# The second part of a fused attention and feed-forward kernel: its last six groups of 256 tokens become three of 512

## The chip, the cores and the metric

The kernel runs on one core of a Trainium2 chip. The metric is the device time of one execution in microseconds (us). Three runs of the kernel before took 733.32, 734.24 and 737.19 us; the median is 734.24. Besides these there is one profiled execution, whose trace is read here. In the trace PE is TensorE's matmul row, PEld its weight loads, DVE is VectorE, ACT ScalarE, POOL GpSimd, SP the engine that issues the DMAs.

## The reference

Causal softmax attention over 4 batches of 8 heads with 576 tokens of 64 is mixed, by a gate per head, with a read-out of a memory matrix. The result, 2304 tokens of 512, goes through a feed-forward layer with a rational activation:

```python
local = softmax(causal(q @ k.T / 8)) @ v
mem_out = (phi(q) @ M_prev) / (phi(q) @ z_prev + 1e-6)      # phi(x) = elu(x) + 1
x = g * mem_out + (1 - g) * local                            # 2304 x 512
h = x @ w_in                                                 # 2304 x 2048
P = a[0] + a[1] * h + a[2] * h**2 + a[3] * h**3
Q = 1.0 + abs(b[0]) * abs(h) + abs(b[1]) * h**2
out = (P / (Q + 1e-6)) @ w_out                               # 2304 x 512
```

## The kernel before, in words

**Precision.** Operands of the large products are split into a high and a low part of a rounded 32-bit type (hi and lo), and a product is three matmuls: hi by hi, hi by lo, lo by hi. The weights arrive as 64-bit floats. `weights` (line 941) turns one 128-row block of a weight, read as pairs of 32-bit words, into hi and lo: an Abs on ScalarE (line 981) into a buffer `wa`, a clamp on VectorE (983), a shift into a PSUM bank (985), a sign step (987), a step that adds the low word's bits and writes a second buffer `wu` (990), then a rounding copy to hi (`rnd`, lines 530 to 532) and a subtraction to lo (`tt`, 519 or 520).

**Two parts of the feed-forward layer.** d_ff is 2048, which is 16 blocks of 128 (the code calls a block `f`). The first part handles blocks 0 to 5 for all nine groups of 256 tokens while attention is still running, and stores the partial sums in DRAM (`po`) and the split tokens in DRAM (`xh`). The second part handles blocks 6 to 15 for the same nine groups; it loads the tokens again (`xagain`, line 1055), and adds the stored partial sum at the end (line 1155). Its weights lie in SBUF that attention gives back; their conversion can begin only then.

**A group.** `group` (line 1073) takes two blocks at a time. `ffn1` (1061) computes h for one block: 12 matmuls with 256 columns (four pieces of d_model by three products) into half of a PSUM bank, so that one bank holds two blocks of 256 tokens. `act_chain` (1003) then works on the full 512 columns: Abs and a linear step on ScalarE, the denominator on GpSimd, Ln and Exp on ScalarE, products on VectorE; it leaves the activation as `gh` and `gl`. `ffn2` (1067) multiplies each 128 tokens of it by w_out: three matmuls with 512 columns. In the second part the groups 0 and 1 take turns, block pair by block pair (`TURNS = 2`), and the others follow one by one.

**The order.** Nothing loops at run time. Every operation is entered in `Sched` with a cost, its reads and writes and a priority; `place` (line 183) puts one after another: of those that can start, the one with the earliest planned start, and of equal starts the one with the lowest priority number. An engine executes its instructions in that order. `c_mm` (line 65) is the planner's price of a matmul. Buffers are counted by tags: `h2` and `o2` allow four PSUM banks for h and four for outputs in the second part, `w` one for conversion; `xg2` has two token buffers, of which one exists as soon as attention has ended and the other as soon as the first part has; `pi` has two buffers for partial sums, `wa2` and `wu2` two each. All DMAs are issued by SP in planned order.

**Priorities in the second part.** A group's chain has 2,000,000 + 5000 per group, its w_in matmuls 4000 less (5000 less in the last group), so that they run ahead as far as the four banks allow; a weight block has 2,000,000 + 5000 per block number, behind the chains of the first groups.

Of the kernel before, what the change touches and what calls it, by code (L numbers as in the profile page):

```python
# [10 lines left out]
F32R = mybir.dt.float32r  # L11
# [51 lines left out]


def c_mm(n, m=128):
    return max(0.4453 * n + 4.0, 0.93 * m)


def c_mm4(n):
# [247 lines left out]
def tile_attention_ffn(  # L317
# [40 lines left out]
    def rb(x):  # L358
        return x.bitcast(F32)
# [101 lines left out]
    for i in range(2):  # L461
        sc.tag(f"g1{i}", 1).free = []

    w1i = [[w1p.tile([128, KC, 128], F32R, name=f"w1i{hl}{f}") for f in range(F0)] for hl in range(2)]
    w1o = [[w1p.tile([128, DM], F32R, name=f"w1o{hl}{f}") for f in range(F0)] for hl in range(2)]
    tags(ffp, "ta", N["ta"], [128, 512])
    tags(ffp, "tb", N["tb"], [128, 512])
    tags(ffp, "tw", N["tw"], [128, 512])
# [472 lines left out]
    def weights(f, wi, wo, p, t3=("xf", "ta", "tw")):  # L941

        for n, dst in (("i", wi), ("o", wo)):
# [17 lines left out]
                return words(), src[1][f * 128:(f + 1) * 128, :]  # L961
            dma(pair, [], [(raw, None)], p, 128 * 2048 * e)
            if wide:
                wa, wu = sc.buf(t3[1]), sc.buf(t3[2])

                def hi32(words=words):
                    return words()[:, 1:1024:2]

                def lo32(words=words):
                    return words()[:, 0:1024:2]  # L970

                def ai(wa=wa):
                    return wa.t.bitcast(I32)

                def ui(wu=wu):
                    return wu.t.bitcast(I32)
                wp = sc.buf("bk", "w")

                def pi(wp=wp):
                    return wp.t.bitcast(I32)  # L980
                act(c_act(512, False), lambda wa=wa, hi32=hi32: A.activation(wa.t, hi32().bitcast(F32), AF.Abs),
                    [(raw, None)], [(wa, None)], p)
                dve(335, lambda wa=wa: V.tensor_scalar(wa.t, wa.t, E_MIN, E_MAX, op0=ALU.max, op1=ALU.min), [], [(wa, None)], p, "1")  # L983

                dve(c_dve(512), lambda ai=ai, pi=pi: V.tensor_scalar(pi(), ai(), 3, 0x3FFFFFF8, op0=ALU.logical_shift_left,
                                                                     op1=ALU.bitwise_and), [(wa, None)], [(wp, None)], p)
                dve(c_dve(512) + 60, lambda pi=pi, hi32=hi32: V.scalar_tensor_tensor(  # L987
                    out=pi(), in0=hi32(), scalar=-(1 << 30), in1=pi(), op0=ALU.bitwise_and, op1=ALU.bitwise_or),
                    [(raw, None)], [(wp, None)], p)
                dve(c_dve(512) + 60, lambda lo32=lo32, ui=ui, pi=pi: V.scalar_tensor_tensor(  # L990
                    out=ui(), in0=lo32(), scalar=29, in1=pi(), op0=ALU.logical_shift_right, op1=ALU.bitwise_or),
                    [(raw, None), (wp, None)], [(wu, None)], p)
                src = wu
            else:
                src = raw
# [56 lines left out]
        dma(lambda: (xh[t0 // 256], rb(xg.t)), [(xg, None)], [(ex("xh"), t0)], p, 128 * KC * 2048)  # L1052
        return xg

    def xagain(tg, t0, p):

        xg = sc.buf(tg)
        dma(lambda: (rb(xg.t), xh[t0 // 256]), [(ex("xh"), t0)], [(xg, None)], p, 128 * KC * 2048)
        return xg

    def ffn1(hb, e, xg, f, p):
        def g():
            return [(hb.t[:, 256 * e:256 * e + 256], WI[wl][f][:, c, :], xg.t[:, xl, c], x == 0 and c == 0, x == 2 and c == KC - 1)
                    for x, (wl, xl) in enumerate([(0, 0), (0, 1), (1, 0)]) for c in range(KC)]
        mm(g, 3 * KC * c_mm(256), [(xg, None), (ex(("wi", f, 0)), None), (ex(("wi", f, 1)), None)], [(hb, e)], p)

# [5 lines left out]

    def group(ts, fs, th, to, tf, tg, p, ahead):

        xg = [(xload(tf, tg, t0, p - 500) if tf else xagain(tg, t0, p - 500)) for t0 in ts]
        ob = [[sc.buf("bk", to) for _ in range(2)] for _ in ts]
        for m in range(0, len(fs), 2):
            for x, o in zip(xg, ob):
# [54 lines left out]
    f_op.deps.update(f1_ops)  # L1133
    f_op.frees = []
    tag2("xf2", N["xf2"], [128, KC, 256], F32, sc.tags["xf"].tiles)
    tag2("xg2", 1, [128, 2, KC, 256], F32R, sc.tags["xg"].tiles)
    tag2("pi", N["pi"], [128, DM])
    tag2("wa2", N["wa2"], [128, 512])
    tag2("wu2", N["wa2"], [128, 512])
    FP2 = 2e6  # L1140
    for f in range(F0, NF):
        weights(f, lambda hl, f=f: WI[hl][f], lambda hl, f=f: WO[hl][f], W2_PRI + pr["w2"] * f, ("xf2", "wa2", "wu2"))
    sc.late(w2_from, LATE["w2"])

    turns = min(TURNS, NG1)
    for g in range(NG1 - turns + 1):
        ts = [256 * x for x in (range(turns) if g == 0 else [g + turns - 1])]
        t0 = ts[0]
        p = FP2 + 5000 * (t0 // 256)
        ob = group(ts, list(range(F0, NF)), "h2", "o2", None, "xg2", p, pr["ahead2" if g < NG1 - turns else "last"])  # L1150
        for ti in range(2 * len(ts)):
            r = t0 + 128 * ti
            pi = sc.buf("pi")
            dma(lambda pi=pi, r=r: (pi.t, po[r:r + 128, :]), [(ex("po"), r)], [(pi, None)], p, 128 * 2048)
            dve(c_dve(512), lambda pi=pi, o=ob[ti]: V.tensor_tensor(out=pi.t, in0=o.t, in1=pi.t, op=ALU.add),
                [(ob[ti], None)], [(pi, None)], p + 900)
            dma(lambda pi=pi, r=r: (out[r:r + 128, :], pi.t), [(pi, None)], [], p + 900, 128 * 2048)
# [6 lines left out]
        PLAN.extend((o.eng, o.start, o.fin - o.lat, o.idx) for o in sc.ops)  # L1164


TURNS = 2

FULL = 6
PLAN = None  # L1170
# [50 lines left out]
```

## Time and profile before

| what | value |
|---|---|
| median of three runs | 734.24 us |
| profiled execution, its own time | 736.42 us |
| its span (first to last instruction) | 734.6 us |
| TensorE matmuls: busy, instructions | 664.3 us (90%), 4113 |
| VectorE | 590.4 us (80%), 1371 |
| ScalarE | 506.5 us (69%), 1121 |
| GpSimd | 461.4 us (63%), 558 |
| mean granted TensorE clock, share of full | 0.981 |
| DMA traffic | 102.56 MB, mean 140 GB/s |

A busy time is the union of the instructions' spans on one engine. Matmuls overlap in the pipeline, so that the duration of one is longer than its distance to the next one's start. The difference between the execution's time and its span lies ahead of the first and behind the last instruction.

### The profile page before, as it was taken

To read this page: it belongs to the slowest core of one execution; us is meant where nothing else is said; L and a number is where in the kernel's file an instruction comes from. 1 tells how busy PE (TensorE), PEld (TensorE's weight loads), DVE (VectorE), ACT (ScalarE), POOL (GpSimd) and SP (SyncE) were. 2 spreads that over 40 slices of the span, in tenths; PEclk is the share of its full clock that TensorE was granted. 3 is DMA by queue.
4 is the path that set the end of the run, shared out by engine and by line. 5 is a ranking of instruction groups with operands and counts; after the bars stand their busy time and mean duration, and the time that the engine had idled before them with its cause. 6 is when DMAs were issued, how large, how long until landed. Compare 5 with 4: busy or idle time off the path is not lost.

```text
span 734.6 us, 12896 instructions
## 1 busy us (share of the span) xinstructions
PE 664.3 (90%) x4113; PEld 578.9 (79%) x4113; DVE 590.4 (80%) x1371; ACT 506.5 (69%) x1121; POOL 461.4 (63%) x558
## 2 busy tenths in 40 slices
PE   3778788998989998889999999878899999999997
PEld 2656567887886777679889998767798998998996
DVE  5787877798999998789789999899775766657674
ACT  3756778789988899879666686575463854755762
POOL 3566656767765786656545887777753745645663
PEclk9999999999999999999999999999999999999999
DMA  6888687846679766764275443612342212212102
GB/s 152 178 202 216 138 204 180 235 112 191 157 168 236 188 162 157 219 159 104 80 260 161 169 159 106 242 61 87 116 124 91 72 62 83 87 58 72 45 9 79
DMA packets 102580, 102.56 MB, mean 140 GB/s; under 512 B 67632, under 2 KB 80432, under 8 KB 100208
## 3 DMA queue, kind: packets, MB, share of 16 engines
q1 hardware_dynamic: 102512, 101.73, 49.7%
q8 instruction: 33, 0.54, 0.3%
q14 instruction: 35, 0.29, 0.1%
HBM read 52.27 MB, written 23.59 MB: 103 GB/s over the span
## 4 chain that ended last, share of the span: by engine, by line
PE 51%; DVE 17%; ACT 11%; DMA 8%; issue 4%; POOL 4%; SPq 4%; DVEq 0%; ACTq 0%; POOLq 0%
PE bk L492 48%; SPq L485 4%; DMA xf<-in_moe_w_in_dram 3%; PE bk L503 3%; DVE bk L704 2%; ACT Ps L708 2%; DVE g L545 2%; ACT P L708 1%; DVE bk L525 1%; DVE gh L525 1%; ACT g L539 1%; DVE bk L987 1%; POOL tw L519 1%; DVE wa L983 1%; DVE wu L990 1%
## 5 line engine op out<-in xcount | busy, mean ns | idle before, releaser
L492 PEld LDWEIGHTS bk<-xg,w2i 128*128 128x128 f32 x1080 | 133.7, 193 | 6.5 <-DVE gl L1038 1.9
L492 PE MATMUL bk<-xg,w2i 128*128 128x256 f32 x1080 | 135.0, 284 | 3.3 <-DVE gl L1038 1.7
L492 PE MATMUL bk<-w2o,gh 128*128 128x512 f32 x360 | 113.3, 396 | 2.9 <-DVE gl L1038 2.9
L1014 ACT ACTIVATE ta<-bk 128x512 f32<-128x512 f32 x72 | 42.9, 596 | 86.7 <-PE bk L492 84.6
L1018 POOL TENSOR_SCALAR tw<-ta,cb 128x512 f32<-128x512 f32 x60 | 48.5, 808 | 83.5 <-ACT ta L1014 83.3
L519 POOL TENSOR_TENSOR tw<-tw,gh 128x512 f32<-128x512 f32 x54 | 70.6, 1307 | 40.6 <-DVE gh L525 39.6
L519 POOL TENSOR_TENSOR tw<-tw,ta 128x512 f32<-128x512 f32 x68 | 89.3, 1316 | 3.8 <-ACT tw L1019 0.3
L492 PE MATMUL bk<-xg,w1i 128*128 128x256 f32 x648 | 84.0, 284 | 0.2
L704 DVE CUSTOM_DVE_ANT_0 bk<-bk,mk 128x512 f32<-128x512 f32 (+3 forms) x144 | 72.7, 518 | 13.4 <-PE bk L492 11.9
L492 PEld LDWEIGHTS bk<-xg,w1i 128*128 128x128 f32 x648 | 80.9, 191 | 2.5 <-DVE g L545 0.8
L492 PEld LDWEIGHTS bk<-w2o,gh 128*128 128x128 f32 x360 | 67.1, 191 | 15.9 <-DVE gl L1038 3.1
L492 PE MATMUL bk<-w2o,gl 128*128 128x512 f32 x180 | 71.6, 398 | 5.7 <-DVE gl L1038 5.7
L1023 DVE TENSOR_TENSOR tb<-bk,tb 128x512 f32<-128x512 f32 x72 | 49.3, 684 | 33.0 <-ACT tb L1015 31.6
L1022 ACT ACTIVATE ta<-tw,lnb 128x512 f32<-128x512 f32 x72 | 52.0, 724 | 32.1 <-POOL tw L519 28.3
L492 PE MATMUL bk<-qk 128*128 128x128 f32 (+3 forms) x256 | 65.5, 360 | 4.3 <-DVE g L545 1.2
L492 PE MATMUL bk<-w1o,gh 128*128 128x512 f32 x216 | 68.7, 399 | 0.0
L525 DVE SCALAR_TENSOR_TENSOR gh<-bk,ca,ta 128x512 fp32r<-128x512 f32 x72 | 53.5, 743 | 18.4 <-ACT ta L1027 15.3
L525 DVE SCALAR_TENSOR_TENSOR bk<-bk,ca,tw 128x512 f32<-128x512 f32 x72 | 54.1, 751 | 14.4 <-POOL tw L519 13.9
L1015 ACT ACTIVATE tb<-bk,ca 128x512 f32<-128x512 f32 x72 | 55.7, 775 | 0.1
L1025 DVE SCALAR_TENSOR_TENSOR bk<-tb,ca,bk 128x512 f32<-128x512 f32 x72 | 53.8, 748 | 1.9 <-ACT ta L1014 1.0
L716 POOL TENSOR_SCALAR st<-st,g 128x1 f32<-128x1 f32 x78 | 24.0, 308 | 48.7 <-ACT Ps L708 41.4
L708 ACT ACTIVATE Ps<-bk,st 128x128 f32<-128x128 f32 (+2 forms) x96 | 46.0, 483 | 10.9 <-DVE st L704 8.1
(152 smaller groups left out, 1623.4 us busy)
## 6 DMA issues: line engine op xcount, KB each, us to landing
qk<-tt SPq DMA_DIRECT2D x32, 384.0 KB, 4.8
xh<-xg SPq DMA_DIRECT2D x9, 1024.0 KB, 4.7
xg<-xh SPq DMA_DIRECT2D x9, 1024.0 KB, 4.8
xf<-in_moe_w_in_dram SPq DMA_DIRECT2D x16, 512.0 KB, 4.4
qk<-tt SPq DMA_DIRECT2D x32, 256.0 KB, 3.6
xf<-in_moe_w_out_dram SPq DMA_DIRECT2D x16, 512.0 KB, 4.8
xs<-x SPq DMA_DIRECT2D x16, 288.0 KB, 2.7
xf<-xs SPq DMA_DIRECT2D x9, 512.0 KB, 5.8
```

Source lines behind the costliest of these rows:

```text
L485: SY.dma_start(out=o, in_=i)
L492: T.matmul(o, lhsT=l, rhs=r, start=s0, stop=s1, skip_group_check=more)
L519: opts = {"pool": ("pool", c_pool2(n), lambda: G.tensor_tensor(**kw()), "t"), "dve": ("dve", c_dve(n), lambda: V.tensor_tensor(**kw()), "2")}
L525: return dve(c_dve(n) + 61 * ap, lambda: V.scalar_tensor_tensor(out=out(), in0=in0(), scalar=scalar() if callable(scalar) else scalar, in1 ...
L704: V.tensor_tensor_reduce(out=s, in0=s, in1=m, scale=-0.125, scalar=st.t[:, 0:1] if x else 3.0e38, op0=ALU.add, op1=ALU.min, accum_out=st.t ...
L708: act(c_act(w, ap=2), lambda bk=bk, w=w, x=x, c0=c0: A.activation(P.t[:, c0:c0 + w], bk.t[:, 0:w], AF.Exp, bias=st.t[:, mx:mx + 1], scale= ...
L1014: act(c_act(N), lambda: A.activation(a_(), h(), AF.Abs), [(hb, None)], [(ta, None)], p)
L1015: sc.op([("act", c_act(N, ap=2), lambda: A.activation(b_(), h(), AF.Identity, scale=ca[:, 3:4], bias=ca[:, 2:3])), ("dve", c_dve(N) + 61, ...
L1018: sc.op([("pool", c_pool(N, 2), lambda: G.tensor_scalar(w_(), a_(), cb[:, 1:2], cb[:, 0:1], op0=ALU.mult, op1=ALU.add), "s"), ("act", c_ac ...
L1022: act(c_act(N, False, 1), lambda: A.activation(a_(), w_(), AF.Ln, scale=2.0 ** -63, bias=lnb[:, 0:1]), [(tw, None)], [(ta, None)], p)
L1023: dve(c_dve(N), lambda: V.tensor_tensor(out=b_(), in0=h(), in1=b_(), op=ALU.mult), [(hb, None)], [(tb, None)], p)
L1025: dve(c_dve(N) + 61, lambda: V.scalar_tensor_tensor(out=h(), in0=b_(), scalar=ca[:, 1:2], in1=h(), op0=ALU.add, op1=ALU.mult), [(tb, None) ...
```

## The change

Of the second part's nine groups, the first three stay narrow (`NARROW = 3`) and the other six become three of 512 tokens. A wide group takes one block at a time: `ffn1w` computes h for 512 tokens with 12 matmuls of 512 columns, whose moving operand is two pieces of 256, into a whole bank, and four `ffn2` follow into four output banks. Its tokens lie in three buffers `xg2` of two 1 MB loads each, which are views of `w1`, now one tile; the loads also wait for the last converted weight. Narrow groups use `xg1`. The fixed turns of groups 0 and 1 are gone. In the weights' conversion of the second part `wu` and `wa` become one buffer (two of them in all), and `pi` has four. The planner's price of a matmul changes for every matmul of the kernel. The priority of the last group's w_in matmuls (`last`) is no longer used, since the last group starts at number 7.

```diff
 def c_mm(n, m=128):
-    return max(0.4453 * n + 4.0, 0.93 * m)
+    return max(0.418 * n + 13.0, 0.93 * m)
...
-    w1i = [[w1p.tile([128, KC, 128], F32R, name=f"w1i{hl}{f}") for f in range(F0)] for hl in range(2)]
-    w1o = [[w1p.tile([128, DM], F32R, name=f"w1o{hl}{f}") for f in range(F0)] for hl in range(2)]
+    w1 = w1p.tile([128, F0, 2, 2, DM], F32R, name="w1")
+    w1i = [[w1[:, f, hl, 0].rearrange("p (c f) -> p c f", c=KC) for f in range(F0)] for hl in range(2)]
+    w1o = [[w1[:, f, hl, 1] for f in range(F0)] for hl in range(2)]
...
-                wa, wu = sc.buf(t3[1]), sc.buf(t3[2])
+                wa = sc.buf(t3[1])
+                wu = wa if t3[2] == t3[1] else sc.buf(t3[2])
...
-    def xagain(tg, t0, p):
+    def xagain(tg, t0, n, p):
         xg = sc.buf(tg)
-        dma(lambda: (rb(xg.t), xh[t0 // 256]), [(ex("xh"), t0)], [(xg, None)], p, 128 * KC * 2048)
+        for e in range(n):
+            dma(lambda e=e: (rb(xg.t[:, e]), xh[t0 // 256 + e]), [(ex("xh"), t0 + 256 * e)] + [(ex(("wo", NF - 1, 1)), None)] * (n - 1), [(xg, e)], p, 128 * KC * 2048)
         return xg
+    def ffn1w(hb, xg, f, p):
+        def g():
+            return [(hb.t.rearrange("p (a b) -> p a b", a=2), WI[wl][f][:, c, :], xg.t[:, :, xl, c], x == 0 and c == 0, x == 2 and c == KC - 1)
+                    for x, (wl, xl) in enumerate([(0, 0), (0, 1), (1, 0)]) for c in range(KC)]
+        mm(g, 3 * KC * c_mm(512), [(xg, None), (ex(("wi", f, 0)), None), (ex(("wi", f, 1)), None)], [(hb, None)], p)
+    def wide_group(t0, n, fs, th, to, tg, p, ahead):
+        x = xagain(tg, t0, n, p - 500)
+        o = [sc.buf("bk", to) for _ in range(2 * n)]
+        for m in range(0, len(fs), 3 - n):
+            hb = sc.buf("bk", th)
+            if n == 2:
+                ffn1w(hb, x, fs[m], p + pr["chain"] * m - ahead)
+            else:
+                for e in range(2):
+                    ffn1(hb, e, x, fs[m + e], p + pr["chain"] * m - ahead, 0)
+            gh, gl = act_chain(hb, 512, p + pr["chain"] * m, True)
+            for k in range(4):
+                f = fs[m + (k // 2 if n == 1 else 0)]
+                ffn2(o[k % (2 * n)], gh, gl, 128 * k, f, f == fs[0], f == fs[-1], p + pr["chain"] * m)
+        return o
...
-    tag2("xg2", 1, [128, 2, KC, 256], F32R, sc.tags["xg"].tiles)
-    tag2("pi", N["pi"], [128, DM])
+    tag2("xg1", 1, [128, 1, 2, KC, 256], F32R, [x.unsqueeze(1) for x in sc.tags["xg"].tiles])
+    tag2("xg2", 0, [128, 2, 2, KC, 256], F32R,
+         [w1[:, 2 * i:2 * i + 2].rearrange("p f h n d -> p (f h n d)").rearrange("p (e h c s) -> p e h c s", e=2, h=2, c=KC)
+          for i in range(F0 // 2)])
+    tag2("pi", 4, [128, DM])
     tag2("wa2", N["wa2"], [128, 512])
-    tag2("wu2", N["wa2"], [128, 512])
...
-        weights(f, lambda hl, f=f: WI[hl][f], lambda hl, f=f: WO[hl][f], W2_PRI + pr["w2"] * f, ("xf2", "wa2", "wu2"))
+        weights(f, lambda hl, f=f: WI[hl][f], lambda hl, f=f: WO[hl][f], W2_PRI + pr["w2"] * f, ("xf2", "wa2", "wa2"))
...
-    turns = min(TURNS, NG1)
-    for g in range(NG1 - turns + 1):
-        ts = [256 * x for x in (range(turns) if g == 0 else [g + turns - 1])]
-        t0 = ts[0]
+    for g in list(range(NARROW)) + list(range(NARROW, NG1, 2)):
+        t0, n = 256 * g, 1 if g < NARROW else 2
         p = FP2 + 5000 * (t0 // 256)
-        ob = group(ts, list(range(F0, NF)), "h2", "o2", None, "xg2", p, pr["ahead2" if g < NG1 - turns else "last"])
+        ob = wide_group(t0, n, list(range(F0, NF)), "h2", "o2", f"xg{n}", p, pr["ahead2" if g < NG1 - 1 else "last"])
...
-TURNS = 2
+NARROW = 3
```

## Rows read from the trace of the kernel before

**Rows 1.** the chain that ended last, 515 to 735: start us, us, what.

```profile
522.55 1.29 POOL w2o L519
523.85 0.77 POOL tw L1018
...
531.86 199.01 PE bk L492 x1258
...
730.89 0.69 DVE pi L1155
```

**Rows 2.** the windows of core 0: busy us (x instructions) by engine, clock, DMA.

```profile
467.00:532.00 65.00, 53.17 (x314) 46.05 (x313) 58.23 (x89) 37.69 (x60) 50.53 (x48) 0.95 0.36 124
532.00:731.00 199.00, 198.85 (x1258) 180.52 (x1258) 133.52 (x196) 115.82 (x179) 110.68 (x98) 1.00 0.21 70
...
480.00:520.00 40.00, 32.81 (x189) 28.53 (x187) 39.68 (x61) 22.58 (x36) 30.21 (x29) 0.96 0.17 54
```

**Rows 3.** groups by line and shape, 532 to 730: busy us, mean ns, idle before.

```profile
L492 PE MATMUL bk<-xg,w2i 128*128 128x256 f32 x816 | 100.6, 283 | 0.0
...
L492 PE MATMUL bk<-w2o,gh 128*128 128x512 f32 x292 | 90.4, 391 | 0.0
L492 PE MATMUL bk<-w2o,gl 128*128 128x512 f32 x147 | 57.4, 391 | 0.9 <-DVE gl L1038 0.9
```

**Rows 4.** the timeline of TensorE at 537 to 549: start us, us, instructions.

```profile
537.23 11.68 PE L492 MATMUL bk<-xg,w2i 128*128 128x256 f32 x96
548.74 0.63 PE L492 MATMUL bk<-w2o,gh 128*128 128x512 f32 x2
```

**Rows 5.** the same timeline at 719 and 730.

```profile
719.13 0.62 PE L492 MATMUL bk<-w2o,gh 128*128 128x512 f32 x2
...
730.01 0.62 PE L492 MATMUL bk<-w2o,gh 128*128 128x512 f32 x2
```

**Rows 6.** the same timeline at 527.

```profile
527.34 3.11 PE L492 MATMUL bk<-xg,w2i 128*128 128x256 f32 x24 [1.31 <-DMA xg<-xh]
```

**Rows 7.** the timeline of all engines, 651 to 664, one activation chain.

```profile
651.63 0.69 DVE L1038 TENSOR_TENSOR gl<-bk,ta 128x512 fp32r<-128x512 f32 x1
...
652.48 0.60 ACT L1014 ACTIVATE ta<-bk 128x512 f32<-128x512 f32 x1 [3.30 <-PE bk L492]
...
661.85 0.68 DVE L1038 TENSOR_TENSOR gl<-bk,ta 128x512 fp32r<-128x512 f32 x1
```

**Rows 8.** timelines of ScalarE, VectorE, GpSimd, 465 to 535: weights being converted.

```profile
477.35 0.68 ACT L981 ACTIVATE wa<-xf 128x512 f32<-128x512 f32 x1 [3.15 <-DMA xf<-in_moe_w_in_dram]
...
480.56 0.69 ACT L981 ACTIVATE wa<-xf 128x512 f32<-128x512 f32 x1
...
506.88 0.67 ACT L981 ACTIVATE wa<-xf 128x512 f32<-128x512 f32 x1
...
515.43 0.68 ACT L981 ACTIVATE wa<-xf 128x512 f32<-128x512 f32 x1 [3.91 <-DVE bk L985]
...
517.44 0.68 DVE L985 TENSOR_SCALAR bk<-wa 128x512 int32<-128x512 int32 x1
...
519.56 0.69 DVE L985 TENSOR_SCALAR bk<-wa 128x512 int32<-128x512 int32 x1
...
500.73 1.30 POOL L519 TENSOR_TENSOR w2i<-wu,w2i 128x512 fp32r<-128x512 f32 x1
...
514.37 1.30 POOL L519 TENSOR_TENSOR w2i<-wu,w2i 128x512 fp32r<-128x512 f32 x1
...
518.31 1.30 POOL L519 TENSOR_TENSOR w2o<-wu,w2o 128x512 fp32r<-128x512 f32 x1
```

**Rows 9.** the line that issues DMAs, 520 to 530.

```profile
L485 SPq DMA_DIRECT2D xg<-xh x2: 327/327/327, 522.6 to 524.0; - x2
...
DMA to landing us min/median/max: 4.6/5.5/6.4
```

**Rows 10.** TensorE's waits, 467 to 532: us in total, times, longest us.

```profile
PE bk L492 <- DVE gl L1038: 10.3, 5, 2.9
```

More of the change, by code (lines that the diff above doesn't have):

```diff
@@ L1053, in xload, with ffn1 @@
         return xg
-    def xagain(tg, t0, p):
+    def xagain(tg, t0, n, p):
         xg = sc.buf(tg)
-        dma(lambda: (rb(xg.t), xh[t0 // 256]), [(ex("xh"), t0)], [(xg, None)], p, 128 * KC * 2048)
+        for e in range(n):
+            dma(lambda e=e: (rb(xg.t[:, e]), xh[t0 // 256 + e]), [(ex("xh"), t0 + 256 * e)] + [(ex(("wo", NF - 1, 1)), None)] * (n - 1), [(xg, e)], p, 128 * KC * 2048)
         return xg
-    def ffn1(hb, e, xg, f, p):
+    def ffn1w(hb, xg, f, p):
         def g():
-            return [(hb.t[:, 256 * e:256 * e + 256], WI[wl][f][:, c, :], xg.t[:, xl, c], x == 0 and c == 0, x == 2 and c == KC - 1)
+            return [(hb.t.rearrange("p (a b) -> p a b", a=2), WI[wl][f][:, c, :], xg.t[:, :, xl, c], x == 0 and c == 0, x == 2 and c == KC - 1)
[16 more added lines that the diff above has]
+        return o
+    def ffn1(hb, e, xg, f, p, half=None):
+        def g():
+            x_ = xg.t if half is None else xg.t[:, half]
+            return [(hb.t[:, 256 * e:256 * e + 256], WI[wl][f][:, c, :], x_[:, xl, c], x == 0 and c == 0, x == 2 and c == KC - 1)
                     for x, (wl, xl) in enumerate([(0, 0), (0, 1), (1, 0)]) for c in range(KC)]
@@ L1073, in group @@
     def group(ts, fs, th, to, tf, tg, p, ahead):
-        xg = [(xload(tf, tg, t0, p - 500) if tf else xagain(tg, t0, p - 500)) for t0 in ts]
+        xg = [xload(tf, tg, t0, p - 500) for t0 in ts]
         ob = [[sc.buf("bk", to) for _ in range(2)] for _ in ts]
@@ L1135, in tile_attention_ffn @@
     tag2("xf2", N["xf2"], [128, KC, 256], F32, sc.tags["xf"].tiles)
-    tag2("xg2", 1, [128, 2, KC, 256], F32R, sc.tags["xg"].tiles)
-    tag2("pi", N["pi"], [128, DM])
+    tag2("xg1", 1, [128, 1, 2, KC, 256], F32R, [x.unsqueeze(1) for x in sc.tags["xg"].tiles])
[3 more added lines that the diff above has]
+    tag2("pi", 4, [128, DM])
     tag2("wa2", N["wa2"], [128, 512])
-    tag2("wu2", N["wa2"], [128, 512])
     FP2 = 2e6
     for f in range(F0, NF):
-        weights(f, lambda hl, f=f: WI[hl][f], lambda hl, f=f: WO[hl][f], W2_PRI + pr["w2"] * f, ("xf2", "wa2", "wu2"))
+        weights(f, lambda hl, f=f: WI[hl][f], lambda hl, f=f: WO[hl][f], W2_PRI + pr["w2"] * f, ("xf2", "wa2", "wa2"))
     sc.late(w2_from, LATE["w2"])
-    turns = min(TURNS, NG1)
-    for g in range(NG1 - turns + 1):
-        ts = [256 * x for x in (range(turns) if g == 0 else [g + turns - 1])]
-        t0 = ts[0]
+    for g in list(range(NARROW)) + list(range(NARROW, NG1, 2)):
+        t0, n = 256 * g, 1 if g < NARROW else 2
         p = FP2 + 5000 * (t0 // 256)
-        ob = group(ts, list(range(F0, NF)), "h2", "o2", None, "xg2", p, pr["ahead2" if g < NG1 - turns else "last"])
-        for ti in range(2 * len(ts)):
+        ob = wide_group(t0, n, list(range(F0, NF)), "h2", "o2", f"xg{n}", p, pr["ahead2" if g < NG1 - 1 else "last"])
+        for ti in range(2 * n):
             r = t0 + 128 * ti
```

## The prediction

> **What bounds the kernel now.** I read from the page to the end of the kernel and then backwards. The busy shares on the page name no single engine, since they are means over stages. The chain of waits does [rows 1]: it ends in one unbroken piece of 199.01 us on TensorE, 531.86 to 730.86, and before that it runs through VectorE, GpSimd and ScalarE. The windows say the same from outside [rows 2]: from 532 to 731 TensorE is busy 198.85 of 199.00 us at full clock, VectorE only 133.52; from 480 to 520 VectorE is busy 39.68 of 40 us and TensorE waits. So the kernel has three stages for this question: up to about 480 the first part and attention; then the conversion of the second part's weights, which VectorE sets; then 199 us that TensorE alone sets. What is saved in TensorE's columns of the last stage comes off the time; what is late in the stage before moves all of it.
>
> The last stage is matmuls of two kinds [rows 3]: 816 with 256 columns (x by w_in) and 292 + 147 with 512 (g by w_out). Mean durations there (283 and 391 ns) overlap and are no price. The price is the distance of starts. 96 of the first kind begin at 537.23 and the next kind at 548.74 [rows 4]: 11.51/96 = 119.9 ns. Of the second, 48 lie between 719.13 and 730.01 [rows 5]: 10.88/48 = 226.7 ns. The records agree: 816 x 0.1199 + 439 x 0.2267 = 197.4 of the 198 us of that view.
>
> **The change, part by part.** *Wide matmuls.* Six groups of 256 tokens, ten blocks of d_ff, 12 matmuls each: 720 with 256 columns become 360 with 512. All 720 lie in TensorE's own stage: seven groups' worth is 840, the first 24 of those run at 527.34 [rows 6] and 816 behind 532 [rows 3]; the changed groups are the last six of the seven. 720 x 119.9 = 86.3 us, 360 x 226.7 = 81.6 us: 4.7 us less. No row has a moving operand in two pieces of 256; the bounds are 226.7 ns (the other 512-column matmul, the same engine and columns, so not less) and 2 x 119.9 = 239.8 (nothing saved). I take 226.7, the nearest in shape.
>
> *Elementwise work.* An activation chain still takes 512 columns, 10 chains for 512 tokens against 2 x 5; the additions to the partial sums and the stores stay 18. Nothing moves here. Cover for a chain's latency: from the first Abs at 652.48 to the end of its last step at 662.53 is 10.1 us [rows 7], and TensorE meanwhile runs four w_in blocks, 11.5 us before, 4 x 12 x 226.7 = 10.9 us after, with an older chain, ended at 652.32, standing in reserve. If the reserve is gone, a change of group costs 12.8 (10.1 and the first block's 2.7) - 10.9 = 1.9 us; three such changes: 0 to 5.7 us. I take 0, because in the 199 us stage the only wait for the last step of a chain is 0.9 us [rows 3].
>
> *Four output banks for one group.* Limits of four stay. A wide group takes all four, so its first w_out matmul waits for the additions of the group before; these lie beside the four w_in blocks just priced. 0; without that cover an addition of 0.69 [rows 1] at each of three changes, 2 us.
>
> *One conversion buffer instead of two.* Weight n may start only when weight n-2 is wholly done. A weight's stay runs from its Abs on ScalarE to the end of its subtraction; the last eight start at 477.35 ... 515.43, up to three in flight; starts and ends are paired from the last backwards [rows 8]. I move each Abs behind the end of the weight two before. The second last (Abs now at 506.88) then waits for 515.67 (514.37 + 1.30); with Abs 0.67 and clamp 0.42 it is ready at 516.8 for its shift on VectorE at 517.44. The last, now at 515.43, moves to 519.61: ready at 520.7 instead of 519.56, so that it ends 1.2 us later, at 525.0. That is a w_out weight, and its first use is behind the chain that releases TensorE at 531.86. For the earlier ones I take the cover that the second last has: VectorE is full from 480 to 520 [rows 2], and a weight waits in its queue anyway. So 0; bounds 0 and +1.2, if the chain is queued behind it on GpSimd (its last subtraction at 522.55, the chain's step at 523.85 [rows 1]).
>
> *Loads.* The wide groups' six loads of 1 MB wait for that last weight, so they are issued from about 525; SP runs them in planned order, and with them stand the four partial-sum loads. Group 2 (still narrow) needs its load, today issued at 522.55, landing in 4.6 us; TensorE waits 1.31 us for it [rows 6, 9]. It was issued as soon as group 0's last w_in block left the buffer, some 2.5 us ahead of the wide ones. So it still goes first: 0. If it goes behind two of them, see the rivals. The first wide pair lands by 525 + 2 x 4.6 = 534.2 while group 2 alone is 120 x 119.9 + 60 x 226.7 ns = 28.0 us of work from 527.3 on.
>
> *Taking turns dropped.* Groups 0 and 1 now go by priority instead of in a fixed alternation. Two input buffers and four output banks still admit just these two before the weights are there, and VectorE sets that stage. 0; bounds: at most the idle time of TensorE there, 65.0 - 53.2 = 11.8 us [rows 2], either way; nearest row: its wait for group 2 of 1.3 us.
>
> *The planner's price of a matmul.* 512 columns fall from 232.0 to 227.0 ns, 256 rise from 119.0 to 120.0; both now equal the distances measured. No instruction changes, but the order of all engines, attention included, is made again by earliest start, so ties fall otherwise. No row prices that. The longest single wait of TensorE in the stage before is 2.9 us [rows 10]; one or two such waits won or lost are my +-4 us, taken as 0.
>
> Sum against the profiled execution: 736.42 (span 734.6) - 4.7 = 731.7. The median of the three runs is 2.18 below the profiled one: 729.5.
>
> **Rivals.** *The wide loads go in front of group 2's.* The Trainium skill, "DMA: Bandwidth & Descriptors", section "Issuing engines are not separate DMA queues", says that transfers share the same 16 engines and interleave. The trace agrees: of the two loads issued at 522.6 and 524.0 one needs 4.6 us, the other 6.4 [rows 9]. As a mechanism of this kernel: two wide loads and then group 2's land at 525.0 + 3 x 4.6 = 538.8 instead of 527.2. TensorE loses the block of 527.34 (2.9 us) and the first new chain then starts from a wide block at 537.2, ready near 537.2 + 2.7 + 10.1 = 550.0 instead of 548.7: 1.3. Together 4.2, and the gain is gone: 733.7, no change. Against it: the 2.5 us of lead; for it: the planner's times are estimates.
>
> *The shared buffer starves the conversion (the other side).* With two in flight the pace is half of a weight's stay. Stays run from 8.4 us (515.43 to 523.84 [rows 1]) to 21.5 (480.56 to 502.03) [rows 8]; the pace now is (523.84 - 477.35)/8 = 5.8. It decides from a stay of 11.6 us. At the middle of the stays, 15, the pace is 7.5 and the eight last weights come 8 x 1.7 = 13.6 us later, and the whole TensorE stage with them: 734.24 - 4.7 + 13.6 = 743. For it: VectorE is full then, and chains have priority. Against: most of a stay is waiting in VectorE's queue, which shrinks when the weight starts later, as the working above shows.
>
> *The wide matmul saves nothing.* Its moving operand lies in two pieces of 256 columns, 8 KB apart, and if each piece pays what a matmul of its own pays, it takes 239.8 ns: 734.2. Against it: no row here shows that a matmul's price depends on how its operand lies, and 512 columns in one piece take 13.1 ns less than twice 256. The Trainium skill, "TensorE: Matmul & The Clock Gate", section "Back-to-back issue gap", speaks against the gain in another way: a warm matmul costs its columns at 2.4 GHz and only 2.5 ns more, so that 360 x (2 x 109.2 - 215.8) = 0.9 us would be saved and the time be 733.3. The trace disagrees: both distances lie some 13 ns over that page's column times, not 2.5.
>
> *The new order of the first part* moves its end by some 4 us: 726 or 734.
>
> **How the numbers follow.** Forecast as summed 0.50 (729.5, own range 727 to 731.5); loads in front 0.15 (733.7); starved conversion 0.11 (738 to 743); nothing saved 0.05 (733 to 734); another order 0.19, half of it to each side (724 to 727, or 733 to 738). 0.5% is 3.7 us, the least that a measurement here can tell from no change. Faster: 0.44 of the forecast and 0.06 of the lucky orders, 0.50. Same: the 0.06 left of the forecast, 0.15, 0.05 and 0.08 of unlucky orders, 0.34. Slower: 0.11 and 0.05, 0.16. The range 724 to 737.5 leaves out the starved case and the tails of the new order.
>
> **What would show it.** w_in matmuls of 512 columns starting 226 to 228 ns apart; the last TensorE piece of the chain again unbroken and still starting within 2 us of 531.9, but 4.7 us shorter (about 194). A second Abs-to-Abs wait for GpSimd's w2 steps would show the shared buffer; a TensorE wait for xg above 3 us near 530 the loads. I am wrong if the piece starts beyond 536, if waits for gl appear inside it at group changes, or if the distance is near 240 ns.

## The result, and the profile after

The changed kernel takes 740.88 us (median of 14 runs, 736.21 to 745.22), the kernel before 733.34 (14 runs, 729.75 to 737.19): the ratio is 1.0104, with a 95% interval of 1.0083 to 1.0124. That is 7.5 us slower, where 4.7 us faster was forecast. The two profiled executions are nearer to each other (738.47 us after, span 736.7; 736.42 before, span 734.6), because the one of before lies above its median and the one of after below; the sums below are made between these two, and the sizes are taken from the runs.

The chain that ended last, in the changed kernel (start us, us, what), answers to [rows 1]:

```profile
520.25 9.37 PE bk L494 x43
...
529.64 4.70 DMA xg<-xh
...
534.48 198.42 PE bk L494 x924
...
732.92 0.69 DVE pi L1184
```

The last piece of TensorE begins at 534.48 instead of 531.86, 2.6 us later, and is 0.6 us shorter, not 4.7. That makes the 2.0 us by which the span grew. Its matmuls run at the pace of the forecast. This is TensorE's timeline (start us, busy us, instructions), one run of wide w_in matmuls and the next kind, to be read as [rows 4, 5] were:

```profile
626.64 11.04 PE L494 MATMUL bk<-w,w2i 128*128 128x512 f32 x48
637.52 0.61 PE L494 MATMUL bk<-w2o,gh 128*128 128x512 f32 x2
```

10.88/48 = 226.7 ns, just the number of the other 512-column matmuls. The Trainium skill, "TensorE: Matmul & The Clock Gate", section "Back-to-back issue gap", gives an isolated warm matmul 2.5 ns over its columns (the figure that the prediction's rival used) and a stream of weight loads and matmuls about 131 ns a matmul at 512 columns. The trace agrees with neither: 226.7 ns is 13.4 over the 213.3 of 512 columns at 2.4 GHz. In the whole piece TensorE waits for nobody. So the saving is there, and the piece is hardly shorter for two other reasons. It has 3.3 us more work when it begins: the first 24 w_in matmuls of group 2, which in the kernel before had run ahead of the piece [rows 6], and two more w_out matmuls (an estimate: 24 x 0.1199 + 2 x 0.2267). And those 24, behind the wait for their tokens, take 538.91 - 534.48 = 4.43 us:

```profile
534.48 4.60 PE L494 MATMUL bk<-xg,w2i 128*128 128x256 f32 x24 [2.73 <-DMA xg<-xh]
538.91 0.63 PE L494 MATMUL bk<-w2o,gh 128*128 128x512 f32 x2
```

In the kernel before they took 530.28 - 527.34 = 2.94 us [rows 6], the next kind starting here:

```profile
530.28 0.63 PE L492 MATMUL bk<-w2o,gh 128*128 128x512 f32 x2
```

The window from 534.5 to 538 us (busy us and instructions of PE, PEld, DVE, ACT, POOL, then the granted clock PEclk, DMA share, GB/s) shows a clock of 0.51, about the lower of its two levels, 1.2 GHz:

```profile
534.50:538.00 3.50, 3.50 (x17) 3.50 (x18) 2.11 (x4) 2.16 (x4) 2.34 (x3) 0.51 1.01 428
```

The groups by line of that stage (busy us, mean ns, idle before), which answer to [rows 3]:

```profile
L494 PE MATMUL bk<-w2o,gh 128*128 128x512 f32 x294 | 90.5, 389 | 0.0
L494 PE MATMUL bk<-w,w2i 128*128 128x512 f32 x360 | 85.0, 389 | 0.0
L494 PE MATMUL bk<-w2o,gl 128*128 128x512 f32 x147 | 57.2, 389 | 0.0
L494 PE MATMUL bk<-xg,w2i 128*128 128x256 f32 x120 | 16.3, 301 | 2.7 <-DMA xg<-xh 2.7
```

The span is 4.7 + 2.0 = 6.7 us longer than forecast: 2.6 + 3.3 = 5.9 us were lost ahead of the piece, and the rest in its first block. The windows of the changed kernel, in the same columns, say where; the last two answer to [rows 2]:

```profile
366.00:464.00 98.00, 98.00 (x624) 89.33 (x623) 89.24 (x131) 63.96 (x104) 66.50 (x61) 1.00 0.48 164
464.00:528.00 64.00, 51.97 (x273) 43.90 (x272) 55.73 (x85) 31.98 (x51) 44.78 (x42) 0.87 0.34 116
...
467.00:532.00 65.00, 52.72 (x286) 44.68 (x285) 53.74 (x83) 33.07 (x53) 43.98 (x42) 0.87 0.33 111
480.00:520.00 40.00, 32.05 (x191) 27.92 (x190) 36.47 (x57) 25.37 (x40) 28.27 (x27) 0.88 0.24 78
```

The first two windows in the kernel before, which are not among its rows:

```profile
366.00:464.00 98.00, 98.00 (x612) 88.72 (x611) 90.89 (x133) 63.36 (x104) 66.34 (x61) 1.00 0.48 165
464.00:528.00 64.00, 53.11 (x317) 46.42 (x316) 57.97 (x88) 36.86 (x58) 49.81 (x47) 0.95 0.38 131
```

Up to 464 us the two are level: what is left of TensorE's work then, at the distances of the prediction, is 248.7 us before (1053 matmuls of 256 columns, 540 of 512) and 243.7 us after (312 and 910), and the 5.0 between them is about the saving of the wide matmuls, 4.7 (an estimate). In the 64 us of the conversion TensorE is busy almost as long (51.97 against 53.11 us) but does 273 matmuls instead of 317, at a mean granted clock of 0.87 instead of 0.95. VectorE, which was full from 480 to 520 (39.68 us), now has gaps (36.47). What the engines waited for between 470 and 535 us (us in total, times, longest), of which the PE lines stand beside [rows 10]:

```profile
PE bk L494 <- DVE gl L1041: 9.7, 3, 4.2
...
ACT wa L984 <- POOL w2o L521: 6.0, 2, 4.3
...
ACT wa L984 <- POOL w2i L521: 5.4, 2, 4.4
...
PE bk L494 <- DMA xg<-xh: 2.7, 1, 2.7
...
PE bk L494 <- POOL w2i L521: 2.1, 2, 1.9
```

TensorE's waits are not much longer in all: 14.5 us in the lines above, 11.6 in the kernel before [rows 6, 10]. So 2.9 of the 6.7 us lost are waits, and the rest, some 4 us (an estimate), is pace. The window that takes in the wait for group 2 and the block behind it, first after, then before:

```profile
464.00:540.00 76.00, 61.24 (x329) 52.53 (x328) 62.89 (x95) 39.52 (x63) 52.02 (x49) 0.87 0.41 147
```

```profile
464.00:540.00 76.00, 64.17 (x384) 55.84 (x383) 66.26 (x100) 42.36 (x66) 55.84 (x52) 0.96 0.37 127
```

With two levels, 1.00 and 0.50, mean clocks of 0.87 and 0.96 say that some 20 of the 76 us ran at the lower level, against 6 before.

The two lines of ACT are the shared conversion buffer: an Abs (now line 984) may start only when a subtraction two weights earlier has ended, 11.4 us of waiting. The last subtraction ends at 528.43 instead of 523.84, and group 2's load goes out at 529.64 instead of 522.55, as the lines of SP show:

```profile
529.64 0.33 SPq L487 DMA_DIRECT2D xg<-xh  x1
530.01 2.04 SPq L487 DMA_DIRECT2D w<-xh  x4
```

### The profile page after: what moved, and what is told of

Its sections match the earlier page's. It is cut to its first block, busy times and chain, and to the rows that moved or that the text cites. A ratio compares the mean times of both kernels' runs of the same rounds, so it can differ in the third digit from the quotient of the medians.

```text
span 736.7 us, 12144 instructions
## 1 busy us (share of the span) xinstructions
PE 665.7 (90%) x3753; PEld 564.5 (77%) x3753; DVE 589.5 (80%) x1370; ACT 503.0 (68%) x1118; POOL 461.2 (63%) x562
## 4 chain that ended last, share of the span: by engine, by line
PE 64%; ACT 10%; DVE 10%; DMA 8%; issue 4%; SPq 2%; POOL 1%; ACTq 0%; DVEq 0%; POOLq 0%
PE bk L494 60%; PE bk L505 4%; SPq L487 2%; DVE bk L706 2%; ACT Ps L710 1%; DMA f<-f 1%; ACT P L710 1%; ACT g L541 1%; DVE g L547 1%; DMA xf<-in_moe_w_out_dram 1%; DMA vz<-in_v_dram 1%; ACT tt L541 1%; DMA qk<-tt 1%; DMA f<-fl 1%; DMA nk<-in_k_dram 1%
## 5 line engine op out<-in xcount | busy, mean ns | idle before, releaser
L494 PE MATMUL bk<-w2o,gh 128*128 128x512 f32 x360 | 115.3, 403 | 0.2 <-DVE gh L527 0.2
L1021 POOL TENSOR_SCALAR tw<-ta,cb 128x512 f32<-128x512 f32 x63 | 50.7, 806 | 70.0 <-ACT ta L1017 69.6
L494 PE MATMUL bk<-xg,w 128*128 128x256 f32 x648 | 83.8, 284 | 2.1 <-ACT f L541 1.3
L494 PE MATMUL bk<-w,w2i 128*128 128x512 f32 x360 | 85.0, 389 | 0.0
L494 PEld LDWEIGHTS bk<-xg,w 128*128 128x128 f32 x648 | 80.6, 191 | 4.0 <-POOL xg L533 1.5
L706 DVE CUSTOM_DVE_ANT_0 bk<-bk,mk 128x512 f32<-128x512 f32 (+3 forms) x144 | 72.6, 517 | 12.2 <-PE bk L494 11.4
L494 PEld LDWEIGHTS bk<-w2o,gh 128*128 128x128 f32 x360 | 69.3, 195 | 14.3 <-DVE gh L527 0.4
L494 PEld LDWEIGHTS bk<-w,w2i 128*128 128x128 f32 x360 | 67.6, 188 | 14.0
L494 PE MATMUL bk<-w,gh 128*128 128x512 f32 x216 | 68.5, 398 | 0.0
L710 ACT ACTIVATE Ps<-bk,st 128x128 f32<-128x128 f32 (+1 forms) x96 | 46.1, 483 | 11.2 <-DVE st L706 9.8
L1030 ACT ACTIVATE ta<-ta,lnb 128x512 f32<-128x512 f32 x72 | 52.0, 722 | 1.1
```

The costliest lines, as they stand in the source:

```text
L494: T.matmul(o, lhsT=l, rhs=r, start=s0, stop=s1, skip_group_check=more)
L706: V.tensor_tensor_reduce(out=s, in0=s, in1=m, scale=-0.125, scalar=st.t[:, 0:1] if x else 3.0e38, op0=ALU.add, op1=ALU.min, accum_out=st.t ...
L710: act(c_act(w, ap=2), lambda bk=bk, w=w, x=x, c0=c0: A.activation(P.t[:, c0:c0 + w], bk.t[:, 0:w], AF.Exp, bias=st.t[:, mx:mx + 1], scale= ...
L1021: sc.op([("pool", c_pool(N, 2), lambda: G.tensor_scalar(w_(), a_(), cb[:, 1:2], cb[:, 0:1], op0=ALU.mult, op1=ALU.add), "s"), ("act", c_ac ...
L1030: act(c_act(N, False, 1), lambda: A.activation(a_(), a_(), AF.Exp, scale=-1.0, bias=lnb[:, 1:2]), [], [(ta, None)], p)
```

## The experiments

The theories changed on the way, as the expectations show. All ratios are to runs of the kernel before on the same chip, with 95% intervals; the clock is the mean granted TensorE clock over a kernel's runs (the kernel before: 0.980 over 129 runs).

| run | median us | ratio | clock |
|---|---|---|---|
| the change | 740.88 | 1.0104 [1.0083, 1.0124] | 0.964 |
| before_new_price | 738.44 | 1.0067 [1.0031, 1.0102] | 0.974 |
| after_old_price | 731.71 | 0.9982 [0.9955, 1.0009] | 0.979 |
| before_shared_buffer | 733.45 | 1.0009 [0.9984, 1.0034] | 0.981 |
| after_with_turns | 739.88 | 1.0094 [1.0064, 1.0124] | 0.971 |
| price_in_attention | 740.77 | 1.0122 [1.0086, 1.0159] | 0.970 |
| price_in_ffn | 744.35 | 1.0150 [1.0116, 1.0185] | 0.971 |
| price_nudged | 737.11 | 1.0052 [1.0032, 1.0072] | 0.977 |
| price_near_the_new_one | 735.05 | 1.0026 [1.0001, 1.0052] | 0.972 |
| changed_nudged | 731.61 | 0.9989 [0.9964, 1.0014] | 0.976 |
| old_price_early_tokens | 728.50 | 0.9941 [0.9920, 0.9963] | 0.978 |
| changed_early_tokens | 749.00 | 1.0227 [1.0187, 1.0268] | 0.961 |
| changed_two_buffers | 738.74 | 1.0093 [1.0061, 1.0125] | 0.969 |
| old_price_early_two_buffers | 735.25 | 1.0030 [1.0003, 1.0057] | 0.976 |
| wide_in_old_order | 728.99 | 0.9933 [0.9907, 0.9959] | 0.981 |
| old_order_at_new_price | 733.02 | 0.9997 [0.9970, 1.0024] | 0.972 |
| old_order_shared_buffer | 729.01 | 0.9943 [0.9918, 0.9969] | 0.982 |
| old_order_new_price_shared | 737.86 | 1.0069 [1.0036, 1.0102] | 0.967 |
| changed_two_buffers_no_tail | 731.71 | 0.9967 [0.9937, 0.9998] | 0.977 |

### One part of the change at a time

The planner's price alone, on the kernel before, and the changed kernel with the old price:

```diff
 # before_new_price; after_old_price is the reverse in the changed kernel
-    return max(0.4453 * n + 4.0, 0.93 * m)
+    return max(0.418 * n + 13.0, 0.93 * m)
```

> The kernel before with only the planner's price of a matmul changed, so that every engine's order is made anew and nothing else. Theory A (the new order of attention and the first part costs the time): slower than before by 0.6 to 1.2%, 738 to 742 us. Theory B (the shared conversion buffer delays the weights) and theory C (the dropped turns): within 0.4% of before.

> The changed kernel with the old price of a matmul. Theory A: the first part ends where it did before (near 464 us of the span) and the wide matmuls show their 4.7 us: 0.3 to 0.8% faster than before. Theory B: the last weight is still converted 4 us or more later than before, and the time stays 0.5 to 1% above before. Theory C: as B, but the late thing is group 2's load, not the weights.

The price alone, with every operation as it was, costs 0.67%, 4.9 us. (The planner also picks the engine of an elementwise step that several engines can do; here ScalarE has one instruction less than before and VectorE one more.) Without the new price the changed kernel is 9.2 us faster, yet not the forecast 4.7 us below before but 1.3, which its interval does not tell from no change.

The shared buffer alone, and the turns put back into the changed kernel:

```diff
 # before_shared_buffer
-        weights(f, ..., W2_PRI + pr["w2"] * f, ("xf2", "wa2", "wu2"))
+        weights(f, ..., W2_PRI + pr["w2"] * f, ("xf2", "wa2", "wa2"))
 # after_with_turns: groups 0 and 1 again alternate, pair by pair
+            ob = turns([0, 256], list(range(F0, NF)), "h2", "o2", "xg1", p, pr["ahead2"])
```

> The kernel before with one conversion buffer tag instead of two in the second part (two tiles in all). Theory A and C: within 0.4% of before, the last subtraction of a weight at 524 to 526 us. Theory B: slower by 0.6 to 1.2%, the last subtraction at 528 or later, with waits of ScalarE's Abs for GpSimd's subtraction.

> The changed kernel, but groups 0 and 1 take turns block pair by block pair again, as before. Theory C: group 2's load is issued within 1 us of the last w_in weight, and the time falls by 3 to 7 us to about before or below. Theory A and B: within 0.4% of the changed kernel, so 0.6 to 1.4% above before.

Neither moves its kernel: +0.09%, and -0.10% against the change. In before_shared_buffer the Abs (there line 982) waits just as long as in the changed kernel, 11.4 us between 470 and 535:

```profile
ACT wa L982 <- POOL w2i L519: 7.0, 2, 3.7
ACT wa L982 <- POOL w2o L519: 4.4, 2, 3.3
```

Yet the window from 464 to 528 us is that of before, 320 matmuls at a clock of 0.95:

```profile
464.00:528.00 64.00, 53.41 (x320) 47.27 (x319) 56.93 (x87) 33.24 (x53) 48.06 (x46) 0.95 0.39 131
```

So ScalarE's waiting by itself costs nothing. That it costs where it meets an order in which somebody waits for that weight is argued, not shown: one buffer also re-makes the plan, and already in before_shared_buffer TensorE's order leaves that of before at matmul 2305 of 4113.

### What about the price: three more prices and two halves

```diff
 # price_in_attention: c_mm new, c_mf (feed-forward layer) at the old price
 # price_in_ffn: c_mm old, c_mf at the new price
+def c_mf(n, m=128): ...
-        mm(g, 3 * KC * c_mm(256), ...)
+        mm(g, 3 * KC * c_mf(256), ...)
 # price_nudged (kernel before) and changed_nudged: 512 columns cost 232.0 ns
+    return max(0.4450 * n + 4.2, 0.93 * m)
 # price_near_the_new_one (kernel before): 227.1 ns for 512 columns, 119.2 for 256
+    return max(0.4217 * n + 11.23, 0.93 * m)
```

> The kernel before; the new price holds only for attention's matmuls, the feed-forward matmuls keep the old one. Where the new price alone costs 0.67% (4.9 us): theory D (attention's new order is what costs) expects 0.4 to 1.0% slower; theory E (the feed-forward blocks get other places) within 0.3% of before; theory F (any new order is a draw, the price has no sign of its own) anything from -0.7 to +1.0%, not adding up with the next kernel to 0.67%.

> The kernel before; the new price holds only for the feed-forward matmuls. Theory D: within 0.3% of before. Theory E: 0.4 to 1.0% slower, the first part's last store at 467 us or later. Theory F: anything from -0.7 to +1.0%.

> The kernel before with a price of 0.4450 n + 4.2 instead of 0.4453 n + 4.0: 512 columns cost 232.04 instead of 231.99 ns in the plan, 256 the same 119.04, so that only ties fall otherwise. Theories D and E: within 0.25% of before. Theory F: away from before by 0.3 to 1.0%, to either side, with about as many other half-clock stretches.

> The changed kernel with the nudged price 0.4450 n + 4.2. If an order is a draw that the first part and attention hold in common with the same price of the kernel before (there +0.52%), and the change itself is worth the -0.18% that it showed at the old price: 734 to 737, +0.2 to +0.5% on before. If the draw is made anew by every change: anything from 728 to 743.

> The kernel before with a third price, 0.4217 n + 11.23: 512 columns cost 227.1 ns in the plan (new price 227.0), 256 columns 119.2 (old 119.0, new 120.0). Of a hundred prices tried it is the one whose plan ends first by the planner's own account. If a cheaper 512-column price as such makes the order worse: 737 to 742, as with the new price. If only the draw of ties counts: 730 to 735, within 0.4% of before.

The halves cost more than the whole (1.22% and 1.50% against 0.67%), a price that differs by 0.05 ns at 512 columns costs 0.52%, and one within 1 ns of the new price 0.26%. So the cost does not follow the value of the price; the price picks an order, and for some elementwise steps an engine (VectorE has 1382 instructions in price_in_ffn and 1371 before). In price_nudged TensorE's order is that of before for the first 2481 of 4113 matmuls, and only the part behind is another. Six orders of the same operations lie from 0 to 1.5%, and that of before is the best of them. One question stays open here: all five new prices lost, and each of the five kernels that ran at both the old and the new price is slower at the new one, by 0.64 to 2.9%. If an order were a blind draw, some should have gained. Either the old price had been picked for its order, or the new one has something against it; no run separates the two. The changed kernel with the nudged price is 0.11% below before instead of 1.04% above.

### Earlier tokens and two buffers: two misses

The third token buffer of 512 tokens becomes two of 256, so that groups 1 and 2 needn't wait for a buffer; and two conversion buffers, for which two partial-sum buffers are given up:

```diff
 # old_price_early_tokens (with the old price), changed_early_tokens
-    tag2("xg1", 1, ..., [x.unsqueeze(1) for x in sc.tags["xg"].tiles])
+    tag2("xg1", 1, ..., [x.unsqueeze(1) for x in sc.tags["xg"].tiles] + [w1[:, F0 - 2 + i]... for i in range(2)])
-          for i in range(F0 // 2)])
+          for i in range(F0 // 2 - 1)])
 # changed_two_buffers; old_price_early_two_buffers has these, the edit above and the old price
-    tag2("pi", 4, [128, DM])
+    tag2("pi", 2, [128, DM])
+    tag2("wu2", N["wa2"], [128, 512])
```

> The changed kernel with the old price, and of the three wide token buffers in the first part's weight space one is cut into two narrow ones, so that group 2's tokens are loaded when the first part ends and not when group 0 is done. If the 2.6 us wait for group 2's load and the half clock behind it are what is left of the lost gain: group 2's load is issued before 500 us, TensorE doesn't wait for it, and the time falls by 2 to 5 us below the changed kernel with the old price (to 727 to 730, 0.4 to 0.8% faster than before). If not, it stays at 731 to 732.5.

> The changed kernel at its own (new) price, with one wide token buffer cut into two narrow ones, so that group 2's tokens come when the first part ends. If the late load of group 2 costs the same in any order, the time falls by about 3 us, as it did at the old price, from 741 to 736 to 739 (0.5 to 0.9% above before). If the loss at this price is the order alone, it stays within 0.3% of the changed kernel, 739 to 743.

> The changed kernel at its own price with two conversion buffer tags again (two tiles each) and, for their space, two partial-sum buffers instead of four. If the shared buffer starves the conversion in this order (Abs waits 4.4 and 4.3 us for a subtraction in its trace): the last subtraction moves from 528.4 to 525 us or earlier and the time falls by 3 us or more, to 738 or less. If not: 739 to 743.

> The changed kernel with the old price, early tokens for group 2, two conversion buffer tags again and two partial-sum buffers. If the shared buffer costs nothing in the old order, 727 to 730 as with the shared one; if it costs its 1 to 2 us there, 725 to 727; if four partial-sum buffers are needed for wide groups, TensorE waits at the two changes between wide groups and the time rises to 730 to 733.

The same edit that gains 0.41% at the old price (0.9982 to 0.9941) loses 1.2% at the new one; in that order TensorE waits 15.3 us for `gl` between 460 and 748 us, and the last subtraction ends at 542 us. Why that order is so bad was not found. The two-buffer runs hardly gained, or lost (old_price_early_two_buffers, 735.25 us, lies above all three of its ranges), and here the trace has a second cause. The end of changed_two_buffers' chain (start us, us, what), and TensorE's last matmul:

```profile
714.97 9.54 PE bk L494 x42
...
724.53 0.70 DVE pi L1185
...
725.25 2.03 DMA out_dram<-pi
...
727.34 2.93 DMA pi<-po
...
730.37 0.69 DVE pi L1185
```

```profile
725.46 0.39 PE L494 MATMUL bk<-w2o,gl 128*128 128x512 f32 x1
```

The chain leaves TensorE at 724.51, with two of the last group's four outputs done; the other two are done at 725.85. Their partial sums are loaded late, the last from 727.34, because a buffer of two comes free only when a result has been stored, and the last addition starts at 730.37, 4.5 us behind TensorE's end (not 5.9, as an expectation below has it, which takes TensorE to end at 724.51). This is a loss that I had put in with `pi`; old_price_early_two_buffers has it too, from 727.96 to 732.44. It hides what the conversion buffer gave.

### The forecast's term by itself, and the four cells

A kernel that has the wide matmuls and nothing else that re-makes the order ahead of them: old price, turns, two conversion buffers; the partial sums of the wide groups lie in the first part's last weight block, so that four fit, their results go into buffers of the activation, and the wide groups' loads wait for group 2's (the diff shows the main lines only):

```diff
 # wide_in_old_order, against the kernel before
+            ob = wide_group(t0, n, ..., f"xg{n}", p, pr["ahead2" if g < NG1 - 1 else "last"])
+    tag2("piw", 0, [128, DM], F32, [rb(w1[:, F0 - 1, i // 2, i % 2]) for i in range(4)])
 # old_order_at_new_price: the same with
+    return max(0.418 * n + 13.0, 0.93 * m)
 # old_order_shared_buffer: the same as wide_in_old_order with one conversion buffer
+        weights(f, ..., ("xf2", "wa2", "wa2"))
 # old_order_new_price_shared: both; changed_two_buffers_no_tail: new price, two buffers, no turns
```

> The kernel before (old price, turns, two conversion buffer tags) with only the last six groups made wide. Their token and partial-sum loads wait for group 2's load, and the partial sums lie in the free weight space, so that every engine's order stays that of the kernel before until group 2 is loaded. Theory F (the wide matmuls give their 4.7 us where the order stays, the rest is a draw of orders): 726.5 to 729.5, 0.4 to 0.8% faster than before. If the wide stage itself loses the gain again: 731.5 to 733.5.

> The kernel wide_in_old_order (wide matmuls, two conversion buffers, turns; ratio 0.9933) with one more edit: the planner's new price of a matmul. Parts that add: the wide matmuls' -0.67% and the price's +0.67% (before_new_price) give 1.000, 733 us. An order drawn anew without a rule: anything from 0.993 to 1.010. Only price and shared conversion buffer together hurt: 0.993 to 1.000, well below the changed kernel's 1.0104 in every case, with no Abs that waits for a subtraction and PE granted over 0.90 between 464 and 528 us.

> wide_in_old_order at the old price with one conversion buffer in place of two. Parts that add: 0.9933 + 0.0009 (before_shared_buffer) = 0.994, 728.5 to 729.5 us. If the shared buffer is what took the gain from after_old_price (0.9982): 0.998, 732.

> wide_in_old_order with both: new price and one conversion buffer, the four cells of price by buffer being complete with it. Parts that add: 1.001, 734 us. The two together hurt, each alone little: 1.008 to 1.010, 739 to 741, with Abs waiting 8 us or more in all for subtractions between 470 and 535 us and a low granted clock (under 0.90) from 464 to 528. A draw without a rule: anything from 0.995 to 1.015.

> The changed kernel at its own price with two conversion buffers, like changed_two_buffers, but with the partial sums of the wide groups in four buffers in the first part's last weight block. changed_two_buffers lost 5.9 us at its end: after TensorE's last matmul (724.51 us) the last partial sum was loaded only when a buffer of two came free, and the last addition ended at 731.1. If the rest of that kernel is as it was: 738.74 - 5.9 = 732.9, ratio 1.001, and the last addition follows TensorE's end at once. If the shared buffer was not what hurt and the order is a draw: 1.005 to 1.015.

In wide_in_old_order TensorE's order is that of before for its first 2997 matmuls, up to the first wide one. It takes 0.67% less than before (interval 0.41 to 0.93%), 4.8 us: the forecast's 4.7. The four cells:

| ratio to before | two conversion buffers | one |
|---|---|---|
| old price | 0.9933 | 0.9943 |
| new price | 0.9997 | 1.0069 |

The price adds 0.64% with two buffers, as it did on the kernel before (0.67%). One buffer adds 0.10% at the old price, as it did there (0.09%), but 0.72% at the new price, and by the two runs without the loss at the end 1.37% in the changed kernel itself (0.9967 against 1.0104; these two also differ in where the partial sums and the third pair of token groups lie and in what the wide loads wait for, and the first came out below its expected 1.001, so that not all of the 1.37% need be the buffer). By the cells, price and buffer together cost 0.62% more than the sum of each alone, with an interval of about 0.56% to either side: only just clear of noise. In old_order_new_price_shared a wait that may make the difference can be seen: TensorE waits once, 6.8 us, for the rounding copy of a late weight (between 460 and 560 us); with two buffers its longest wait there is 2.1 us.

```profile
PE bk L494 <- POOL w2i L533: 6.8, 1, 6.8
PE bk L494 <- DMA xg<-xh: 4.1, 2, 2.1
```

The low clock that was expected with it isn't there:

```profile
464.00:528.00 64.00, 52.07 (x295) 44.62 (x294) 56.59 (x85) 32.13 (x50) 42.67 (x40) 0.95 0.29 99
```

And one buffer re-makes the order here too, from matmul 2314 on; that this order is slower by chance, and not by the lost buffer, is not ruled out.

The three fastest, wide_in_old_order (0.9933), old_price_early_tokens (0.9941) and old_order_shared_buffer (0.9943), beat the kernel before and the changed one, and the measurement can't tell them apart. All three have the old price.

## Why the prediction was wrong

*Wide matmuls, -4.7 us: right.* Pace 226.7 ns, no wait in the last piece, and 4.8 us by the run that has them alone.

*Elementwise work, output banks, turns, each 0: right.* TensorE waits for no `gl` behind 534.48, and the turns are worth 0.10% at the new price, inside the interval.

*Loads, 0: the order was right, the size was not.* Group 2's load goes ahead of the wide ones, by 0.4 us and not 2.5. But it came 7 us later than I had it, and the wide ones 5, since what they wait for was later; TensorE waits 2.7 us instead of 1.3, and the block behind the wait is slow. At the old price, where the wait for that load is 2.6 us, earlier tokens are worth 0.41% (after_old_price to old_price_early_tokens, an interval of about 0.35% to either side), 3 us.

*The planner's price, taken as 0 with +-4: this step failed.* It is worth +0.64 to +0.67%, 4.7 to 4.9 us, on two kernels (intervals of about 2.7 us to either side), enough to eat the whole saving, and 1.22%, 9.0 us, in the changed kernel itself, far beyond the bound I gave it. I had sized it by "one or two such waits won or lost" of the conversion stage; two waits of 2.9 us would already have been 5.8. And the order of the matmuls differs from the 43rd on, and the bound of an edit that re-makes everything isn't the longest wait of one stage. In the changed kernel's profile the loss lies between 464 and 540 us; that its first part sends off its last partial sum later (467.86 us instead of 463.91) is no loss by itself, since as much work is done by 464. Where the price alone loses its 4.9 us, and by which tie, stays open: the profiled execution of before_new_price has a span only 0.9 us longer than that of before (735.5 and 734.6).

*The shared buffer, taken as 0 with +1.2: right alone, wrong in company, as far as the runs tell.* My cover for it was "VectorE is full from 480 to 520, and a weight waits in its queue anyway" [rows 2, 8]. That is a fact of the old order. In the new one VectorE has 3.5 us of gaps there, and one buffer, whose 11.4 us of waiting cost nothing on the kernel before, goes with a loss of 0.72 to 1.37%, 5 to 10 us, under the new price. That the lost cover is the reason is argued, not shown. My rival of the starved conversion had the waiting (743 us, chance 0.11) and took it for a matter of pace. That its range, 738 to 743 us, holds the measured 740.88 is luck in good part: without the new price the same buffer costs 0.10%.

The sum by the runs: -4.9 (wide) + 4.8 (price) + 5.3 to 10.0 (one buffer under that price) = +5.2 to +9.9 us; measured +7.5. Its last term comes from other kernels, so that it fits loosely. A plainer sum stays with the changed kernel: at the old price it is 0.18% below before, -1.3 us, the late load of group 2 having taken, by old_price_early_tokens, some 3 of the 4.7; the new price adds 1.22%, +9.0; together +7.7. Two rivals that I had as alternatives seem to have come true together, and the range ended at 737.5, because I added up terms that were each worked out in the order of before while one of them changed that order.

The prediction's signs spoke only in part. The piece starts 2.6 us later (within 2 was asked) and is 198.42 us long, not 194; but none of the three signs of being wrong appeared: it does not start beyond 536, TensorE waits for no `gl` inside it, and the distance is not near 240 ns. All three watched the last stage, and most of the loss (5.9 of 6.7 us) lay ahead of it. One slip besides: "another order" got a chance of 0.19, half to each side, but enters the sums with 0.06 and 0.13.

## What to carry to other kernels

An edit to a planner's costs is an edit to the whole program: measure it by itself, on unchanged instructions, and expect a change of the size that other near-equal prices give (here 0.26 to 1.5%, all of them losses). A cost that is "hidden by" something is hidden in one order only; if the same change re-makes the order, its hidden costs can come back as open ones. And an experiment that frees a resource by taking another one away should be read from the end of its chain first, or its second loss is taken for the answer.

## What the runs showed of the hardware

The time goes with TensorE's granted clock more than I expected. Over the kernel before's 129 runs, one program, the time falls by 2.9 us for each 0.01 of mean clock (correlation -0.65); in other kernels the correlation goes from none (+0.05, after_old_price, 12 runs) to -0.96 (old_order_new_price_shared, 10 runs). The kernels at the new price have mean clocks of 0.961 to 0.977, those at the old price 0.976 to 0.982. The change has 0.964 against 0.980, which by that slope would be 4.7 of its 7.5 us (an estimate). How such a stretch looks in the changed kernel, by its windows and by TensorE's timeline:

```profile
505.00:517.50 12.50, 10.59 (x70) 9.56 (x69) 11.22 (x20) 7.62 (x13) 10.57 (x11) 1.00 0.26 85
517.50:524.30 6.80, 4.90 (x13) 3.31 (x12) 6.76 (x13) 1.86 (x3) 4.03 (x5) 0.50 0.00 1
524.30:534.50 10.20, 7.47 (x51) 6.60 (x49) 5.31 (x8) 4.49 (x7) 7.55 (x8) 1.00 0.38 138
```

```profile
516.80 0.74 PE L494 MATMUL bk<-xg,w2i 128*128 128x256 f32 x4 [1.91 <-POOL w2i L521]
517.38 0.97 PE L494 MATMUL bk<-w2o,gh 128*128 128x512 f32 x2
520.25 0.80 PE L494 MATMUL bk<-w2o,gl 128*128 128x512 f32 x1 [1.90 <-DVE gl L1041]
520.84 1.05 PE L494 MATMUL bk<-w2o,gh 128*128 128x512 f32 x2
521.70 0.63 PE L494 MATMUL bk<-w2o,gl 128*128 128x512 f32 x1
522.12 1.05 PE L494 MATMUL bk<-w2o,gh 128*128 128x512 f32 x2
522.98 0.63 PE L494 MATMUL bk<-w2o,gl 128*128 128x512 f32 x1
```

TensorE has waited 1.91 us for a weight of the shared buffer; from 517.5 to 524.3 it is granted 0.50, the lower level of 1.2 GHz, and waits another 1.90 us, for `gl`, within that stretch. At this level three matmuls of 512 columns take 522.12 - 520.84 = 1.28 us, 427 ns each instead of 226.7. If the clock falls because of the wait, a wait costs more than its own length. But whether a lower clock makes the times or both follow from the waits no run here separates; that a wait brings the low level is argued from such rows, not shown.
